# Chunk bounds of a top-k attention: PSUM transposes by TensorE replaced by 32x32 block transposes on VectorE

## The chip, the cores and the metric

The kernel runs on one core of a Trainium2 chip. The metric is device time of the whole program in microseconds (us), the median of several runs. TensorE is PE in the profile (PEld is its weight load), VectorE is DVE, ScalarE is ACT, GpSimd is POOL, and SyncE, which here issues DMAs, is SP.

## What is computed

An attention in which each query may look at six chunks of 32 keys only, followed by a gated feed-forward layer. There are 4 batches of 8 heads, 768 tokens, a head size of 64, so 24 chunks a head.

```
k_min = np.min(k_chunks, axis=3); k_max = np.max(k_chunks, axis=3)
ub = np.sum(np.maximum(q * k_min, q * k_max), axis=-1)      # per query and chunk
ub = np.where(causal, ub, -1e9)                            # chunk <= the query's own
top_chunks = np.argsort(ub, axis=-1)[..., -6:]
scores = where(selected chunk and causal, scale * q @ k.T, -1e9)
attn_out = softmax(scores) @ v
x = attn_out as (3072, 512); xn = x / rms(x) * g
out = (silu(xn @ w_gate) * (xn @ w_val)) @ w_out           # d_ff 1536
```

The bound of a chunk is written as `q . k_min + relu(q) . (k_max - k_min)`, which is two matrix products.

## The kernel before, and what sets its order

The kernel works on 16 pairs of heads, four to a batch. For a pair, k and q are loaded (`knat`, `qnat`), transposed on TensorE in fp32 ("pk" and "pq") and copied out of PSUM by ScalarE or VectorE ("kt", "qt"). VectorE reduces k over each chunk to a minimum and a maximum (`red`), their difference is taken (`diff`), and both are the stationary operand `KU` of the bounds. `relu` makes the second moving operand ("rt").

The bounds ("ub") are fp32 products of 64 rows by 32 columns, placed in the array by `tile_position`. The first four pairs (`DUO = 4`) do them one by one in `prep`: the 768 tokens are laid as three groups of 256 on three 32-column groups. Later pairs go two at a time through `duo`: four groups of 384 tokens, two for each pair. Either way a chunk's bounds then lie along partitions and tokens along the free axis. They are copied to SBUF by ScalarE or VectorE (step "ubE", tiles "ubs" and "ubd"), turned on TensorE against an identity (step "up"), and VectorE adds the causal table `cmf` (24 chunks for each token tile and head) while it takes them out of PSUM (step "ubm").

`choose` follows: twelve `max` a pair for the eight largest bounds, then two instructions that write a 0/1 selection. For pairs 0 to 3 the selection is transposed on TensorE ("st", step `selT`) and copied to `QS` by ScalarE or VectorE; later pairs write it beside q into `QN`, and two transposing DMAs from SP bring both into `QS`. The selection is extra rows of the query operand, so the score product ("sc") masks by itself. Then come exp on ScalarE ("pt"), the product with v ("av"), and VectorE's division ("xb"). When a batch's pairs are done, `norm` scales half a batch of rows ("xs", after a GpSimd power, "ri"); the first half is transposed on TensorE ("tp") and copied by ScalarE ("xT"), the others by DMA. `ffn` then runs twelve blocks of gate ("gp") and value ("vp") products and the output product ("po").

The order on each engine is not written out by hand. Every piece of work is a `Step` with an assumed cost, dependences and buffers; `Order.run` plays them through and gives an engine that is free the ready step of lowest rank. A rank is a sum of entries of `TIMES` (by pair, score block, norm and feed-forward half) and `RANK` (by kind of step). The program is then emitted in that order, and each engine works strictly down its own list. TensorE's list also has 88 "busy" products of zeros (lines 343 to 351, and 923 in `scores`), which stand where `Order.run` found nothing else to do. PSUM has eight buffers; `limits` says how many of them each sort of work may hold.

Of the kernel before, what the change touches and what calls it, by code (L numbers as in the profile page):

```python
# [21 lines left out]
GUARD = 480.0  # L22
# [5 lines left out]
        av=317.13, dif=-371.68, eps=-127.03, exp=38.25, kC=146.63, kE=47.74, kT=-378.59,  # L28
        kload=5.92, kmn=-649.18, kmx=-154.73, max=-339.88, qC=211.54, qE=806.71, qT=255.12,
        qload=7.58, relu=-70.96, root=214.18, sc=306.41, sel=71.38, selC=354.68, selT=-82.52,  # L30
        sq=-533.35, tp=81.74, tpE=457.86, ub=-353.85, ubE=-844.2, ubm=-100.58, up=-547.88,
        vload=-466.13, xT=41.94, xb=-434.88, xs=291.71,
    ),
    dict(
        av=-67.94, dif=-197.08, eps=-1181.62, exp=65.8, gate=-45.76, hh=-195.3, kC=431.48,
        kE=188.25, kT=-156.35, kload=309.73, kmn=365.65, kmx=725.58, mask=148.9, max=122.37,
        out=-321.42, po=568.17, poE=255.36, qE=-143.72, qN=503.6, qT=46.14, qX=-360.16,
        qload=286.61, relu=311.95, root=-959.29, sc=-163.03, sel=639.07, sq=-56.05, tanh=845.43,
        tg=-155.94, ub=-92.79, ubE=-119.4, ubm=322.89, up=-194.73, val=-19.16, vload=289.68,
        xT=31.48, xb=-144.92, xs=-231.75,  # L40
# [161 lines left out]
def kernel(  # L202
# [26 lines left out]
    G = 3  # L229
    DUO = 4  # L230
    KSIDE, QM = 16, 4
    HW = NT * P + D
    NPAIRS = B * NP

    SLOTS = dict(ps=8, nat=7, kb=0, qn=2, vext=4, set=3, ku=4, selq=2, qt=7, ubs=1, ubd=1, small=8, ubm=3,
# [6 lines left out]
    BOUNDS = ("ACT", "DVE")  # L242
# [78 lines left out]
    cmf = const.tile([P, NT, 2, NCH], FP32, name="cmf")  # L321
# [92 lines left out]
    def make_cmf(n):  # L414
        if n == 0:
            nc.gpsimd.memset(cmf[:], 0.0)
        for g4 in (2 * n, 2 * n + 1):
            nc.gpsimd.affine_select(
                out=cmf[32 * g4:32 * (g4 + 1)], in_=cmf[32 * g4:32 * (g4 + 1)],
                compare_op=ALU.is_ge, fill=-BIGC,  # L420
                base=g4, pattern=[[4, NT], [0, 2], [-1, NCH]], channel_multiplier=0,
            )

    c_cm = add("cmf", "POOL", 1.5, -70, lambda e: make_cmf(0), [c_e])
    c_cm = add("cmf", "POOL", 1.1, -69, lambda e: make_cmf(1), [c_cm])
# [61 lines left out]
    def prep(c, i0, nb, at, lr):  # L487
# [162 lines left out]
        def choose(last, ubm, m8):  # L650
            for j in range(0, nb, 3):
                def top(e, j=j):
                    if m8.tile is None:
                        tile_of(m8, [P, 2, NT, 8] if side_q else [P, NT, 2, 8], FP32, "m8")
                    for x in range(j, j + 3):
                        for h in range(2):
                            y = (h, x) if side_q else (x, h)
                            nc.vector.max(out=m8.tile[:, y[0], y[1], :],  # L658
                                          in_=ubm.tile[:, y[0], y[1], 0:max(8, 4 * (i0 + x) + 4)])

                last = add("max", "DVE", 0.33 + 0.05 * j, rank(at, b, "max", j, "step"), top, last, opens=[m8], uses=[ubm])
                last = [last]
            sq = None if side_q else Buf("selq")

            def pick(e):
                if side_q:
                    if side_q:
                        s12 = QN[qn.slot][:, D:D + 2 * NT * P].rearrange("p (t d) -> p t d", d=P)
                        m12, um = (x.tile[:].rearrange("p h i e -> p (h i) e") for x in (m8, ubm))
                    else:  # L670
                        s12 = SELQ[sq.slot][:, 0:nb].rearrange("p i h e -> p (i h) e")
                        m12, um = (x.tile[:, 0:nb].rearrange("p i h e -> p (i h) e") for x in (m8, ubm))
                    nc.vector.scalar_tensor_tensor(
                        out=s12[:, :, 0:NCH], in0=m12[:, :, 5:6].to_broadcast([P, 2 * nb, NCH]),
                        scalar=THRFLOOR, in1=um, op0=ALU.max, op1=ALU.is_gt)
                    nc.vector.tensor_scalar(
                        out=s12[:, :, NCH:NCH + 1], in0=m12[:, :, 0:1], scalar1=-GUARD,
                        scalar2=0.0, op0=ALU.add, op1=ALU.max)
                    return
                s12 = SELQ[sq.slot][:, 0:nb].rearrange("p i h e -> p (i h) e")  # L680
                m12 = m8.tile[:, 0:nb].rearrange("p i h e -> p (i h) e")
                nc.vector.scalar_tensor_tensor(
                    out=s12[:, :, 0:NCH],
                    in0=m12[:, :, 5:6].to_broadcast([P, 2 * nb, NCH]),
                    scalar=THRFLOOR, in1=ubm.tile[:, 0:nb].rearrange("p i h e -> p (i h) e"),
                    op0=ALU.max, op1=ALU.is_gt)
                nc.vector.tensor_scalar(
                    out=s12[:, :, NCH:NCH + 1], in0=m12[:, :, 0:1], scalar1=-GUARD,
                    scalar2=0.0, op0=ALU.add, op1=ALU.max)
# [26 lines left out]
        if p >= DUO:  # L716
            c.bound = (big["q"], rel), [rl] + [c.dif[x] for x in c.dif], choose
            return

        nq = n // G  # L720
        nj = nq // P
        ub = [Buf("ps", "prep") for _ in range(2)]
        ubs = Buf("ubs")

        def bounds(e):
            t = [tile_of(x, [P, 2 * P], FP32, "ub") for x in ub]
            for m, src in ((0, big["q"].tile), (1, rel.tile)):
                for g in range(G):
                    for h in range(2):
                        rows = slice(h * D, (h + 1) * D)  # L730
                        nc.tensor.matmul(  # L731
                            t[h][g * CH:(g + 1) * CH, 0:nq], KU[c.ku.slot][rows, m, :],
                            src[rows, g * nq:(g + 1) * nq],
                            start=(m == 0), stop=(m == 1), tile_position=(h * D, g * CH))

        um = add("ub", "PE", 0.25 + 0.8 * nq / 256, rank(at, b, "ub"), bounds,
                 [rl, df] + [c.dif[x] for x in c.dif], opens=ub,
                 uses=[c.ku, big["q"], rel])
        ue = []
        for h in range(2):  # L740
            def ub_out(e, h=h):
                if ubs.tile is None:
                    tile_of(ubs, [G * CH, 2, 2 * P], FP32, "ubs")
                evict(e, ubs.tile[:, h, 0:nq], ub[h].tile[0:G * CH, 0:nq])

            ue.append(add("ubE", "", {e: {"ACT": act(nq), "DVE": dve(nq)}[e] for e in BOUNDS},
                          rank(at, b, "ubE", h, "step"), ub_out, [um], opens=[ubs],
                          uses=[ub[h]]))
        up, ubm, m8 = Buf("ps", "prep"), Buf("ubm"), Buf("small")

        def up_turn(e):
            t = tile_of(up, [P, G, nj, 2, CH], FP32, "up")
# [406 lines left out]
```

## Time and profile before

| | us |
|---|---|
| runs | 317.39, 317.07, 317.8 (median 317.39) |
| profiled execution, first to last instruction (span) | 315.0 |
| busy TensorE / VectorE / ScalarE / GpSimd | 307.8 / 232.9 / 193.3 / 105.9 |

The profiled execution is known by its span; what a run takes around it is the difference to the runs. In a group of instructions the columns are line, engine, operation, tiles, shapes and count, then the busy time of the group in us and the mean of one instruction in ns, then the engine's idle time before them and what ended it. In the chain of waits a piece has its start, its length, the engine, tile and line, and how many instructions it merges. In the timeline a piece has start, length, engine, line, operation, shapes, count, and in brackets the idle time before it. TensorE's instructions are pipelined: the mean of one holds the way through the array, so that the distance between neighbours in the chain, not that mean, is what each costs. The granted TensorE clock was 1.000 in the whole span.

### The profile page before, as it was taken

The page shows a single profiled execution, that of the slowest core. Times are in us where ns is not written, and L with a number is a line of the kernel's source. Part 1 is how long each engine was busy: PE and PEld are TensorE (multiplying, and loading weights), DVE is VectorE, ACT ScalarE, POOL GpSimd, SP SyncE. Part 2 cuts the span into 40 slices and gives each one's busy share as a digit, 9 for nine tenths or more (in the row PEclk, how much of TensorE's full clock was granted, in tenths as well). Part 3 has the DMA queues.
Part 4 walks back from the last instruction along what each step waited for, and adds up shares of the span by engine and source line. Part 5 has one row for each costly group of instructions (what it writes and reads, how often), then busy time and mean ns, then how long its engine had stood idle before and what let it go on. Part 6 is the DMA issues. An engine that isn't in the chain of part 4 may idle for free.

```text
span 315.0 us, 7610 instructions
## 1 busy us (share of the span) xinstructions
PE 307.8 (98%) x2820; PEld 195.9 (62%) x2820; DVE 232.9 (74%) x654; ACT 193.3 (61%) x417; POOL 105.9 (34%) x160
## 2 busy tenths in 40 slices
PE   8989999899999999999999999999999999999995
PEld 4567788566667654776766667556666546555542
DVE  7679999898965964996899959558776928844600
ACT  4689997747289773479866599954348423423131
POOL 8684636017345752104802667510001200000000
PEclk9999999999999999999999999999999999999999
DMA  8999995998979997999472566650000151001023
GB/s 169 219 207 198 203 148 85 175 145 108 137 113 183 127 100 198 234 184 216 118 50 51 86 91 80 143 143 35 0 2 0 37 147 54 2 33 67 2 85 115
DMA packets 113333, 35.36 MB, mean 112 GB/s; under 512 B 106256, under 2 KB 110096, under 8 KB 113296
## 3 DMA queue, kind: packets, MB, share of 16 engines
q1 hardware_dynamic: 83184, 26.62, 42.1%
q0 software_dynamic: 28512, 7.87, 26.7%
q10 hardware_dynamic: 1600, 0.39, 0.6%
q8 instruction: 22, 0.36, 0.5%
q14 instruction: 15, 0.12, 0.2%
HBM read 28.57 MB, written 6.29 MB: 111 GB/s over the span
## 4 chain that ended last, share of the span: by engine, by line
PE 97%; ACT 2%; issue 0%; DVE 0%; ACTq 0%
PE gp L1045 20%; PE po L1086 20%; PE vp L1066 20%; PE sc L876 12%; PE av L912 7%; PE busy L346 5%; PE pk L525 4%; PE pq L525 3%; PE ub L789 3%; PE ub L731 1%; PE up L811 1%; ACT pt L893 1%; PE sc L882 1%; PE up L755 0%; PE st L702 0%; ACT xT L297 0%
## 5 line engine op out<-in xcount | busy, mean ns | idle before, releaser
L893 ACT ACTIVATE pt<-sc 128x512 bf16<-128x512 f32 (+3 forms) x192 | 87.8, 583 | 4.6 <-PE sc L876 2.8
L1052 ACT ACTIVATE sg<-gp 128x384 bf16<-128x384 f32 x96 | 47.3, 500 | 58.2 <-PE gp L1045 53.0
L1045 PE MATMUL gp<-xT,wg 128*128 128x384 bf16 x384 | 74.6, 326 | 0.9 <-ACT xT L297 0.9
L1066 PE MATMUL vp<-xT,wv 128*128 128x384 bf16 x384 | 74.8, 326 | 0.0
L1058 DVE SCALAR_TENSOR_TENSOR tg<-sg,gp 128x384 bf16<-128x384 bf16 x96 | 51.7, 548 | 21.8 <-ACT sg L1052 20.0
L1086 PE MATMUL po<-wo,hh 128*128 128x512 bf16 x288 | 66.5, 379 | 0.0
L1074 DVE TENSOR_TENSOR hh<-vp,tg 128x384 bf16<-128x384 f32 x96 | 51.2, 549 | 6.8 <-PE vp L1066 5.5
L876 PE MATMUL sc<-qs,ke 128*128 128x128 bf16 (+5 forms) x420 | 52.7, 251 | 0.1
L1045 PEld LDWEIGHTS <-wg 128*128 128x128 bf16 x384 | 36.8, 98 | 24.4 <-issue 1.7
L1066 PEld LDWEIGHTS <-wv 128*128 128x128 bf16 x384 | 36.5, 98 | 24.0 <-issue 0.6
L1086 PEld LDWEIGHTS <-hh 128*128 128x128 bf16 x288 | 27.5, 98 | 29.4
L899 POOL TENSOR_SCALAR_AFFINE_SELECT pt<-pt 128x512 bf16<-128x512 bf16 (+1 forms) x48 | 25.7, 552 | 57.3 <-ACT pt L893 57.2
L876 PEld LDWEIGHTS <-ke 128*128 128x128 bf16 (+1 forms) x420 | 30.5, 97 | 12.4 <-issue 2.1
L301 POOL CAST ke<-kt 64x768 bf16<-64x768 f32 x31 | 26.2, 846 | 26.9 <-ACT kt L297 15.1
L912 PE MATMUL av<-vx,pt 128*128 128x65 bf16 x672 | 32.5, 193 | 0.2 <-ACT pt L893 0.2
L912 PEld LDWEIGHTS <-pt 128*128 128x128 bf16 x672 | 28.7, 97 | 5.8 <-issue 0.3
L299 ACT ACTIVATE osb<-po 128x512 f32<-128x512 f32 x22 | 13.3, 606 | 29.7 <-PE po L1086 29.6
L989 DVE SCALAR_TENSOR_TENSOR xs<-xb,ri,gains 128x512 bf16<-128x512 bf16 x24 | 19.1, 835 | 5.6 <-DMA xT<-xs 5.1
L346 PE MATMUL busy<-zeros 128*128 128x512 bf16 (+1 forms) x88 | 18.7, 351 | 1.3 <-DVE zeros L341 1.3
L933 DVE TENSOR_TENSOR xb<-av,rden 128x384 bf16<-128x384 f32 (+1 forms) x34 | 18.1, 534 | 1.2
L481 POOL DMA_DIRECT2D vx<-in_v_dram x16 | 16.7, 1045 | 0.5 <-PE gp L1045 0.3
L658 DVE MAX8 m<-ubm 128x8 f32<-128x8 f32 (+2 forms) x192 | 16.8, 156 | 0.0
(85 smaller groups left out, 296.8 us busy)
## 6 DMA issues: line engine op xcount, KB each, us to landing
out_dram<-osb SPq DMA_DIRECT2D x24, 256.0 KB, 2.3
knat<-in_k_dram SPq DMA_DIRECT2D x30, 192.0 KB, 4.5
qnat<-in_q_dram SPq DMA_DIRECT2D x30, 192.0 KB, 4.7
vx<-in_v_dram POOLq DMA_DIRECT2D x16, 192.0 KB, 5.9
wg<-in_moe_w_gate_dram POOLq DMA_DIRECT2D x2, 768.0 KB, 9.0
wv<-in_moe_w_val_dram POOLq DMA_DIRECT2D x2, 768.0 KB, 10.8
wo<-in_moe_w_out_dram POOLq DMA_DIRECT2D x2, 768.0 KB, 8.4
ke<-e_all SPq DMA_DIRECT2D x4, 96.0 KB, 2.9
```

What stands on the lines that cost most here:

```text
L301: engine[e].tensor_copy(out_, in_)
L346: nc.tensor.matmul(t[:, 0:n], zeros[:, 0:P], zeros[:, 0:n], start=True, stop=True)
L876: nc.tensor.matmul(t[:, x:x + m, :].rearrange("p a b -> p (a b)"), ke[kk, kb * P:(kb + 1) * P], qs[kk, q0 * P:(q0 + m) * P], start=not tri ...
L893: nc.scalar.activation(out=t[:, 0:nn, :], in_=sc.tile[:, 0:nn, :], func=ACT.Exp, scale=SCALE)
L899: nc.gpsimd.affine_select(out=pt.tile[:, 0:nd, :], in_=pt.tile[:, 0:nd, :], compare_op=ALU.is_ge, fill=0.0, base=0, pattern=[[0, nd], [1, ...
L912: nc.tensor.matmul(av.tile[:, qi - i0, :], pt.tile[:, x, :], VX[c.v.slot][:, hl * NT + kb, :], start=(begin and m == 0), stop=(left[0] == ...
L1045: nc.tensor.matmul(t[:], wg[:, g, hs], XT[b].tile[:, g, cols], start=(g == 0), stop=(g == NP - 1))
L1052: nc.scalar.activation(out=t[:], in_=gp.tile[:], func=ACT.Tanh, scale=0.5)
L1058: nc.vector.scalar_tensor_tensor(out=t[:], in0=sg.tile[:], scalar=1.0, in1=gp.tile[:], op0=ALU.add, op1=ALU.mult)
L1066: nc.tensor.matmul(t[:], wv[:, g, hs], XT[b].tile[:, g, cols], start=(g == 0), stop=(g == NP - 1))
L1074: nc.vector.tensor_tensor(out=t[:], in0=vp.tile[:], in1=tg.tile[:], op=ALU.mult)
L1086: nc.tensor.matmul(po.tile[:], hhs[ht].tile[:, th * P:(th + 1) * P], wo[:, ht, :], start=(ht == 0), stop=(ht == NHT - 1))
```

## The change

Both ways of doing the bounds become one function, `bound`, called for a single pair (0 to 3) or for two. A column group `a` of the array now takes the tokens whose place in their 128-token tile is `32a` to `32a + 31`: the moving operand is read as six runs of 32 tokens, and the 32 chunks (24 and 8 zeros) of column group `a` land on partitions `32a` to `32a + 31` of PSUM. A transpose of each 32x32 block, which VectorE does while it reads PSUM, puts tokens on partitions and chunks on the free axis. The copies to SBUF and TensorE's turns go. The causal add is done in SBUF afterwards, only on eight chunks for each token tile: from the tile's first chunk on; what lies behind them is never looked at by the maxima, and masked later by the causal score blocks. `cmf` shrinks to eight columns. All values of `RANK` and `TIMES` are new.

```diff
-    cmf = const.tile([P, NT, 2, NCH], FP32, name="cmf")
+    cmf = const.tile([P, 8], FP32, name="cmf")
...
-    def make_cmf(n):
-        if n == 0:
-            nc.gpsimd.memset(cmf[:], 0.0)
-        for g4 in (2 * n, 2 * n + 1):
+    def make_cmf(e):
+        nc.gpsimd.memset(cmf[:], 0.0)
+        for g4 in range(4):
...
-                base=g4, pattern=[[4, NT], [0, 2], [-1, NCH]], channel_multiplier=0,
+                base=g4, pattern=[[-1, 8]], channel_multiplier=0,
...
+    def bound(cs):
+        at, b, nx = f"a{cs[-1].p}", cs[0].b, len(cs)
+        ub, ubm = [Buf("ps", "prep") for _ in range(2)], Buf("ubm")
+        side_q = cs[0].p >= QM
+        def bounds(e):
+            t = [tile_of(y, [P, nx, UW], FP32, "ub") for y in ub]
+            for m in range(2):
+                for x, c in enumerate(cs):
+                    for a in range(4):
+                        for h in range(2):
+                            rows = slice(h * D, (h + 1) * D)
+                            nc.tensor.matmul(
+                                t[h][a * CH:(a + 1) * CH, x, :].rearrange("p (t r) -> p t r", r=CH),
+                                KU[c.ku.slot][rows, m, :],
+                                c.bound[0][m].tile[rows, :].rearrange(
+                                    "d (t a r) -> d a t r", a=4, r=CH)[:, a],
+                                start=(m == 0 and x == 0), stop=(m == 1 and x == nx - 1),
+                                tile_position=(h * D, a * CH))
...
+        for h in range(2):
+            def turn(e, h=h):
...
+                if side_q:
+                    o, i = ubm.tile[:, :, h * UW:(h + 1) * UW], ub[h].tile[:]
+                else:
+                    o = ubm.tile[:, 0].rearrange("p (t h c) -> p h t c", h=2, c=CH)[:, 1 - h]
+                    i = ub[h].tile[:, 0].rearrange("p (t c) -> p t c", c=CH)
+                nc.vector.transpose(out=o, in_=i)
...
+        def causal(e):
+            for x in range(nx):
+                w = ubm.tile[:, x, 0:8]
+                w = bass.AP(w.tensor, w.offset, [
+                    w.ap[0], (UW if side_q else CH, 2), ((CH if side_q else 2 * CH) + 4, NT), (1, 8)])
+                nc.vector.tensor_tensor(
+                    out=w, in0=w, in1=cmf[:].rearrange("p (a b w) -> p a b w", a=1, b=1).to_broadcast(
+                        [P, 2, NT, 8]), op=ALU.add)
```

Here `UW` is 192 and `CH` is 32. The removed parts are the ub, ubE, up and ubm steps at the end of `prep` and the whole of `duo`, which stand above. `choose` and `pick` read the new layout (32 columns a tile and head, of which 24 are used) and keep their instructions.

More of the change, by code (lines that the diff above doesn't have):

```diff
@@ L228 @@
     W = S // 2
-    G = 3
     DUO = 4
@@ L232 @@
     HW = NT * P + D
+    UW = NT * CH
     NPAIRS = B * NP
-    SLOTS = dict(ps=8, nat=7, kb=0, qn=2, vext=4, set=3, ku=4, selq=2, qt=7, ubs=1, ubd=1, small=8, ubm=3,
+    SLOTS = dict(ps=8, nat=7, kb=0, qn=2, vext=4, set=3, ku=4, selq=2, qt=7, small=8, ubm=3,
                  pt=10, xb=2, xt=2, row=3, xs=4, ff=8, hh=31, ob=3)
@@ L420, in make_cmf @@
                 compare_op=ALU.is_ge, fill=-BIGC,
[L421 removed]
+                base=g4, pattern=[[-1, 8]], channel_multiplier=0,
             )
[L424 to L425 removed]
+    c_cm = add("cmf", "POOL", 0.8, -70, make_cmf, [c_id])
     def make_tri(e):
@@ L647, in prep, with choose @@
                  uses=[big["q"]], port=True)
-        def choose(last, ubm, m8):
+        def choose(last, ubm, x, m8):
             for j in range(0, nb, 3):
@@ L653, in top @@
                     if m8.tile is None:
-                        tile_of(m8, [P, 2, NT, 8] if side_q else [P, NT, 2, 8], FP32, "m8")
-                    for x in range(j, j + 3):
+                        tile_of(m8, [P, 2 * NT, 8], FP32, "m8")
+                    for i in range(j, j + 3):
                         for h in range(2):
[L657 to L662, printed above, removed]
+                            y = h * NT + i if side_q else 2 * i + h
+                            nc.vector.max(out=m8.tile[:, y, :],
+                                          in_=ubm.tile[:, x, y * CH:y * CH + max(8, 4 * i + 4)])
+                last = [add("max", "DVE", 0.33 + 0.05 * j, rank(at, b, "max", j, "step"), top, last,
+                            opens=[m8], uses=[ubm])]
             sq = None if side_q else Buf("selq")
@@ L714, in choose @@
             return fin
[L716 to L723, printed above, removed]
-        def bounds(e):
[L726 to L739, printed above, removed]
-        for h in range(2):
[L741 to L748, printed above, removed]
@@ L749, in prep @@
-        up, ubm, m8 = Buf("ps", "prep"), Buf("ubm"), Buf("small")
-        def up_turn(e):
-            t = tile_of(up, [P, G, nj, 2, CH], FP32, "up")
-            for j in range(nj):
-                for h in range(2):
-                    nc.tensor.transpose(
-                        t[:, :, j, h if side_q else 1 - h, :], ubs.tile[:, h, j * P:(j + 1) * P],
-                        ident_f[0:G * CH, 0:G * CH])
-        ut = add("up", "PE", 0.083 * 2 * nj, rank(at, b, "up"), up_turn, ue, opens=[up], uses=[ubs])
@@ new lines, in prep @@
+        c.bound = (big["q"], rel), [rl] + [c.dif[x] for x in c.dif], choose
+    def bound(cs):
+        at, b, nx = f"a{cs[-1].p}", cs[0].b, len(cs)
+        ub, ubm = [Buf("ps", "prep") for _ in range(2)], Buf("ubm")
+        side_q = cs[0].p >= QM
+        def bounds(e):
+            t = [tile_of(y, [P, nx, UW], FP32, "ub") for y in ub]
[11 more added lines that the diff above has]
+                                tile_position=(h * D, a * CH))
+        um = add("ub", "PE", 0.35 + 0.64 * nx, rank(at, b, "ub"), bounds,
+                 [y for c in cs for y in c.bound[1]], opens=ub,
+                 uses=[y for c in cs for y in (c.ku,) + c.bound[0]])
+        turns = []
+        for h in range(2):
+            def turn(e, h=h):
+                if ubm.tile is None:
+                    tile_of(ubm, [P, nx, 2 * UW], FP32, "ubm")
+                if side_q:
+                    o, i = ubm.tile[:, :, h * UW:(h + 1) * UW], ub[h].tile[:]
+                else:
+                    o = ubm.tile[:, 0].rearrange("p (t h c) -> p h t c", h=2, c=CH)[:, 1 - h]
+                    i = ub[h].tile[:, 0].rearrange("p (t c) -> p t c", c=CH)
+                nc.vector.transpose(out=o, in_=i)
+            turns.append(add("ubT", "DVE", 0.08 + nx * UW * 0.00106, rank(at, b, "ubT", h, "step"), turn,
+                             [um], opens=[ubm], uses=[ub[h]]))
+        def causal(e):
+            for x in range(nx):
[5 more added lines that the diff above has]
+                        [P, 2, NT, 8]), op=ALU.add)
+        last = add("ubm", "DVE", 0.27 * nx, rank(at, b, "ubm"), causal, turns + [c_cm], uses=[ubm])
@@ L826, in duo @@
         for x, c in enumerate(cs):
-            c.bound[2](done[x], ubms[x], Buf("small"))
+            c.bound[2]([last], ubm, x, Buf("small"))
     GROUPS = {
@@ L1109 @@
         load_v(c, f"l{p}")
[L1110 to L1120 removed]
+        pairs.append(c)
+        if p >= DUO and p % 2 == 0:
+            continue
+        group = pairs[-2:] if p >= DUO else [c]
+        bound(group)
+        for c in group:
+            for i0, nb in PARTS[c.p]:
+                scores(c, i0, nb, f"s{c.p}.{i0}", f"pace{min(b, 1)}", b == 0)
     for b in range(B):
```

113 lines of the change are left out of this document (17 added, 96 removed), and 30 rows, old and new, of the table TIMES.

## The prediction

> **What bounds the kernel now.** I read the page's busy shares and its chain first.
>
> ```profile
> span 315.0 us, 7610 instructions
> PE 307.8 (98%) x2820; PEld 195.9 (62%) x2820; DVE 232.9 (74%) x654; ACT 193.3 (61%) x417; POOL 105.9 (34%) x160
> PE 97%; ACT 2%; issue 0%; DVE 0%; ACTq 0%
> ```
>
> The chain that ended last is TensorE almost from end to end, so a microsecond taken from TensorE's instructions comes off the time, unless TensorE then waits instead. The timed runs are 317.39 us (median); the profiled execution spans 315.0, and the 2.4 us around the span are kept as they are. A busy share doesn't tell whether TensorE does useful work, so next come its waits, the stretch before and after the first gate product (58.03 us), and the stretches around it.
>
> ```profile
> PE busy L346 <- DVE zeros L341: 1.3, 1, 1.3
> PE gp L1045 <- ACT xT L297: 0.9, 1, 0.9
> PE pk L525 <- ACT pt L893: 0.9, 1, 0.9
> 0.00:58.03 58.03, 54.84 (x656) 39.33 (x657) 50.28 (x168) 45.70 (x95) 36.02 (x58) 1.00 1.08 173
> 58.03:315.00 256.97, 253.00 (x2164) 156.57 (x2163) 182.62 (x488) 147.60 (x322) 69.87 (x102) 1.00 0.62 99
> 40.00:50.00 10.00, 10.00 (x164) 8.36 (x170) 9.69 (x24) 9.07 (x20) 4.50 (x6) 1.00 0.75 109
> ```
>
> The columns after the stretch are PE, PEld, DVE, ACT and POOL. After 58.03 TensorE lacks 4 us of 257: there its work alone sets the time. Before 58.03 it is different: part of its work is filler (L346 multiplies zeros; all 88 fillers stand before the first gate product in both built orders), and VectorE is at 97% from 40 to 50. I call this stretch the head. What a shorter TensorE list is worth there depends on VectorE.
>
> **The change part by part, on TensorE.** The transposes called "up" go altogether. Matrix products of the bounds ("ub") keep their columns in the six joint steps and are laid out anew in the four single ones.
>
> ```profile
> L811 PE MATMUL up<-ident_f,ubd 128*128 128x128 f32 x36 | 5.2, 274 | 0.0
> L755 PE MATMUL up<-ident_f,ubs 96*128 96x96 f32 x16 | 2.0, 248 | 0.0
> 53.47 0.66 PE up L811 x6
> 11.69 0.33 PE up L755 x4
> 49.30 1.45 PE ub L789 x32
> 9.66 1.01 PE ub L731 x24
> ```
>
> Instructions overlap, so their cost is read from the chain: 0.11 us for each of the 36 and 0.083 for each of the 16, which makes 3.96 + 1.33 = 5.3 us. Each bounds instruction leaves two records. A joint step has 32 records of 384 columns, eight abreast, so four turns, in 1.45 us; a single one 24 of 256 columns, six abreast, four turns, in 1.01. The difference of 0.44 over 4 x 128 columns gives 0.86 ns a column and turn, and 0.13 us besides. The new single step has 16 instructions of 192 columns, eight abreast: four turns, 0.13 + 4 x 192 x 0.00086 = 0.79 us, 0.22 less, four times 0.9. The new joint step has 32 instructions of 192: eight turns of half the length, 1.45 again. In sum 5.3 + 0.9 = 6.2 us of TensorE. The reads step through the tokens in runs of 32; a stepped operand costs nothing in the nearest rows, so I count none:
>
> ```profile
> L882 PE MATMUL sc<-trimask,ident_b 128*128 128x512 bf16 x6 | 2.3, 380 | 0.0
> L876 PE MATMUL sc<-qs,ke 128*128 128x512 bf16 x30 | 9.4, 379 | 0.0
> ```
>
> By the list of instructions, 2.1 us of the 6.2 lie in the head (16 small transposes, the first joint step's six, the four single steps, less 0.7 of score and projection work moved forward) and 4.0 behind it.
>
> Bounds on the 6.2: if 192 columns are too short to hide the issue of twice the instructions, each of the new 256 costs what the shortest product does in the chain, about 0.031 us ("av" with 65 columns, row further down: four in 0.12); 7.9 us, less than the 11.9 that the turns already take (4 x 0.79 + 6 x 1.45), so the gain stays 6.2. If each of their 512 records costs it, ub is 15.9 and the gain falls to 2.2.
>
> **On VectorE, ScalarE and GpSimd.** Evictions of the bounds and the adds from "up" go; 32x32 transposes from PSUM and small adds come.
>
> ```profile
> L818 DVE TENSOR_TENSOR ubm<-up,cmf 128x144 f32<-128x144 f32 x24 | 6.4, 295 | 0.0
> L770 DVE TENSOR_TENSOR ubm<-up,cmf 128x288 f32<-128x288 f32 x4 | 1.8, 449 | 0.1
> L301 DVE COPY ubd<-ub 128x384 f32<-128x384 f32 x6 | 3.3, 554 | 3.5 <-PE ub L789 3.4
> L301 DVE COPY ubs<-ub 96x256 f32<-96x256 f32 x3 | 1.3, 419 | 2.4 <-PE ub L731 2.4
> L297 ACT ACTIVATE ubd<-ub 128x384 f32<-128x384 f32 x6 | 2.9, 491 | 3.5 <-PE ub L789 3.5
> L297 ACT ACTIVATE ubs<-ub 96x256 f32<-96x256 f32 x5 | 1.8, 399 | 2.7 <-PE ub L731 2.7
> L418 POOL TENSOR_SCALAR_AFFINE_SELECT cmf<-cmf 32x288 f32<-32x288 f32 x4 | 2.0, 507 | 0.3
> ```
>
> VectorE loses 24 x 0.295 + 4 x 0.449 + 6 x 0.554 + 3 x 0.419 = 13.5 us. No row shows a VectorE transpose. From below it costs what a copy of the same tile does, 0.554 for 384 columns; the two adds give 1.07 ns an element and 0.14 besides, so 0.35 for 192. From above I take two passes, 0.95 and 0.55. I take the copy's price, its nearest row: 12 x 0.554 + 8 x 0.35 = 9.4. The add over eight chunks has 96 elements, 0.24 by the same line, 16 of them 3.9. Sum 13.3: VectorE gains nothing, and ScalarE is freed of 4.7 us. GpSimd's causal table shrinks from 2.0 us and a memset to five tiny instructions, early in the head. The max and selection instructions keep their counts and sizes, and no DMA is added or removed on any queue.
>
> **The head.** Up to the first "xs" of the norm, VectorE's list is as long as before: over four single steps and the first joint one it gets 8 x 0.35 + 2 x 0.554 + 6 x 0.24 = 5.3 us and loses 3 x 0.419 + 4 x 0.449 + 0.554 = 3.6 (the old joint adds stood behind xs). In the new order two copies of the chunk pattern come to it from ScalarE (about 0.55 each, as a copy of that width), and four copies of transposed k and q (0.55 each) and one relu leave it. So this engine gives the head no microsecond, TensorE's list 2.1 at most. The last part of the head can be followed in these rows:
>
> ```profile
> 48.79 0.29 PE L912 MATMUL av<-vx,pt 128*128 128x65 bf16 x4
> 53.18 2.08 DVE L989 SCALAR_TENSOR_TENSOR xs<-xb,ri,gains 128x512 bf16<-128x512 bf16 x3 [0.40 <-POOL ri L981]
> 55.34 1.30 PE busy L346 x8
> 56.47 0.61 PE L1011 MATMUL tp<-ident_b,xs 128*128 128x128 bf16 x8
> 56.90 1.09 ACT xT L297 x2
> 48.50 0.12 PE av L912 x4
> ```
>
> From the last "av" to the gate it takes 9.24 us. The rows of xs end at 55.26, yet the eight fillers queued ahead of the last "tp" hold it until 56.47. The new order has its fillers ahead of all twelve tp. VectorE has there, ahead of xs, two transposes and two adds (1.3 us with their overlap) where one copy stood (0.5); after xs come tp and the third of three ScalarE copies, about 1.1 us later. Sum: 4.4 to the start of xs, plus 0.8, plus 2.1, plus 1.1: 8.4. So 0.8 is gained there, and of the 1.1 us of shorter work ahead of the last av I take 0.4, as VectorE is nearly full. Head: 1.2, between 0 and 2.1.
>
> **Sum.** 4.0 + 1.2 = 5.2: span 309.8, time 317.39 - 5.2 = 312.2. Its own range: 311.2 (all 6.2) to 313.9 (3.5, with a few short waits).
>
> **Rivals.** *VectorE's leg grows longer than TensorE's work beside it (slower).* Place: the selection turns ("st") of the four single pairs, which TensorE meets in its order and which nothing can pass. For pair 3 the built order, its pieces priced as in the chain, leaves 4.6 us of TensorE work from the bounds' start to st, where it was 6.7; for pair 0 6.2 against 7.2. VectorE's leg after the bounds, in rows:
>
> ```profile
> 11.52 0.56 DVE L301 COPY kt<-pk 128x384 f32<-128x384 f32 x1 [0.31 <-PE pk L525]
> 12.51 0.94 DVE L556 TENSOR_REDUCE ku<-kt 128x24 f32<-128x768 f32 x1
> 13.37 0.51 DVE L658 MAX8 m<-ubm 128x8 f32<-128x8 f32 x6
> 14.65 0.57 DVE L658 MAX8 m<-ubm 128x8 f32<-128x16 f32 x6
> 15.26 1.06 DVE L682 SCALAR_TENSOR_TENSOR selq<-m,ubm 128x288 bf16<-128x288 f32 x1
> L687 DVE TENSOR_SCALAR selq<-m x4: 184/200/811, 16.2 to 38.3; 128x12 bf16<-128x12 f32 x4
> ```
>
> For pair 3: two transposes 0.7, add 0.24, two copies 1.1, twelve max 1.1, a reduce 0.94, selection 0.64 in its fast form (0.45 is the least of L682): 4.7, and 0.8 for the bounds with 0.2 to be seen: 5.7, so 1.1 us of waiting. Where the selection's two instructions run long (1.06 and 0.81) it is 1.2 more. Four pairs at 1.7 are 6.8: 312.2 + 6.8 = 319.0. It decides from 1.3 us a pair; two-pass transposes add 0.4 to each. For it: the order is tighter at all four. Against: TensorE waited for no st before, and the list ahead of each has fillers only in part.
>
> *VectorE alone sets the head.* The evacuation went from two engines to one; with 9.69 of 10 busy, the head then shortens by nothing: 317.4 - 4.0 = 313.4. The Trainium skill says in TensorEngine Tiling (Array Packing), section PSUM Bottleneck, that packing speeds up TensorE but not the emptying of PSUM, and asks for ScalarE and VectorE both. By that rule the time is this rival's; the 97% row bears it out, the 50.28 busy of 58.03 in the whole head does not.
>
> *Weight loads show.* Twice the turns need twice the loads.
>
> ```profile
> L789 PEld LDWEIGHTS ub<-qt,ku 64*32 64x32 f32 x96 | 1.1, 104 | 1.3 <-issue 0.5 <-DVE xs L989 0.4 <-DVE ubm L818 0.2
> ```
>
> If each of the 24 added turns shows its 0.104 us load, 2.5 come back: 314.7. Against it, 0.13 us is all that a joint step of four turns has beside its columns. The Trainium skill, in TensorE: Matmul & The Clock Gate, section Part 3: Packing small matmuls, has a load overlap a running product only when its row group differs, which these turns of the same tiles would break; the trace disagrees at 384 columns by that 0.13.
>
> *The weights for the value product are late.* It follows the gate by 1.3 us in the new order, by 4.5 before.
>
> ```profile
> 49.19 0.78 POOL L445 DMA_DIRECT2D wv<-in_moe_w_val_dram  x1 [0.20 <-issue]
> 62.58 1.63 PE L1066 MATMUL vp<-xT,wv 128*128 128x384 bf16 x9
> DMA to landing us min/median/max: 9.2/10.8/12.4
> ```
>
> Issued at 49.2 and landing after 9.2 to 12.4, it comes between 58.4 and 61.6; wanted at 58.1 (gate at 56.8), it costs 0.3 to 3.5: up to 315.7.
>
> **How the numbers follow.** Forecast 0.54; slower legs 0.19; VectorE's head 0.11; weight loads 0.04; late weights 0.07; all of it cancelling 0.05. About 0.2% (0.6 us) is what a measurement of this kernel tells from no change. Faster: 0.54 + 0.11 + 0.04 + 0.07 = 0.76; same 0.05; slower 0.19. The likeliest time is 312.2; the range runs from 309.3, should the head also lose its 0.9 us waits and some filler time, to 318.0, which leaves out the upper half of the slower case.
>
> **What would show it.** Right: no "up", TensorE busy less by about 6 us, ub at 1.45 and 0.8 in the chain, first gate near 56.8, TensorE's waits below 4 us. Wrong: transposes above 0.95, waits at st of a microsecond each, vp waiting for a DMA, or score products waiting for their transposed selection behind 58 us, which now rest on a wholly new order and which no row can exclude.

## The result, and the profile after

| | us |
|---|---|
| before, five runs | 317.44 (317.07 to 317.8) |
| after, five runs | 315.27 (314.38 to 317.29) |
| ratio after to before | 0.9939, 95% interval 0.9919 to 0.9959 |
| predicted | 312.2 (309.3 to 318.0) |

The kernel is faster, by 2.2 us where 5.2 were predicted. The profiled execution of after is the slowest of its five (span 315.5, the others 312.7 to 313.6), so its span isn't to be set against the 315.0 of before, and its stretches show what can happen behind the gate rather than what usually does. First the page's busy line, the chain by engines and the waits of TensorE (us in all, how often, the longest):

```profile
span 315.5 us, 7918 instructions
PE 305.1 (97%) x2992; PEld 194.8 (62%) x2992; DVE 232.3 (74%) x653; ACT 189.7 (60%) x406; POOL 102.0 (32%) x160
PE 88%; DMA 5%; DVE 3%; ACT 1%; POOL 0%; SPq 0%; issue 0%; ACTq 0%; DVEq 0%; POOLq 0%
```

```profile
PE av L836 <- POOL pt L823: 2.5, 1, 2.5
PE sc L800 <- ACT qs L296: 1.0, 1, 1.0
PE gp L969 <- ACT xT L296: 0.9, 1, 0.9
PE st L686 <- DVE ubm L735: 0.4, 1, 0.4
```

TensorE's share of the chain fell from 97% to 88%: DMA and VectorE now hold 8% of it, and there is a new stop of 2.5 us. Where these lie is seen by stretches, cut at the first gate product (58.05, before 58.03) and around the stop. Behind the stretch and its length stand the busy times of PE, PEld, DVE, ACT and POOL, then the granted clock, the DMA share and GB/s:

```profile
0.00:58.05 58.05, 54.01 (x705) 38.72 (x705) 48.08 (x156) 45.59 (x94) 34.73 (x61) 1.00 1.09 172
58.05:315.50 257.45, 251.08 (x2288) 156.12 (x2287) 184.25 (x499) 144.08 (x312) 67.24 (x99) 0.99 0.62 99
```

```profile
94.00:95.00 1.00, 1.00 (x17) 0.60 (x14) 0.20 (x1) 0.74 (x2) 0.08 (x1) 0.77 0.66 151
95.00:98.00 3.00, 3.00 (x12) 1.52 (x11) 1.11 (x2) 2.09 (x5) 1.89 (x3) 0.51 1.18 243
98.00:99.00 1.00, 1.00 (x15) 0.74 (x13) 0.56 (x1) 0.49 (x1) 0.00 (x0) 1.00 1.52 172
```

So the head kept its length, and behind it TensorE stands 6.4 us where it stood 4.0, and runs at half its clock for about 3.4 us after the stop: 0.23 + 3 x 0.49 = 1.7 us lost.

**The parts, as the chain and the groups show them.**

```profile
9.33 0.81 PE ub L714 x32
51.60 1.46 PE ub L714 x64
```

```profile
L735 DVE STREAM_TRANSPOSE ubm<-ub 128x384 f32<-128x384 f32 x12 | 6.3, 560 | 2.7 <-PE ub L714 2.7
L735 DVE STREAM_TRANSPOSE ubm<-ub 128x192 f32<-128x192 f32 x8 | 2.6, 384 | 2.1 <-PE ub L714 2.1
L745 DVE TENSOR_TENSOR ubm<-ubm,cmf 128x96 f32<-128x96 f32 x16 | 4.2, 290 | 0.2
L671 DVE TENSOR_SCALAR selq<-m x4: 189/742/814, 14.8 to 38.2; 128x12 bf16<-128x12 f32 x4
```

The bounds cost 0.81 and 1.46 us a step. The transposes cost about what a copy does (0.560 us in the mean for 384 columns, where the copy of before had 0.554, and 0.384 for 192). The three figures of the last row are least, median and most in ns. This instruction (L671, here called the guard) is the second of the two that write the selection. It changed without being touched: its median was 200 ns and is 742.

**The head.** The last "av" ahead of the norm and the first gate product, in the timeline:

```profile
49.90 0.29 PE L836 MATMUL av<-vx,pt 128*128 128x65 bf16 x4
58.05 1.46 PE L969 MATMUL gp<-xT,wg 128*128 128x384 bf16 x8 [0.93 <-ACT xT L296]
```

From av to gate it is 8.15 us (9.24 before), but av is 1.1 us later (48.79 before). To see where that is lost, take the last of the four turns of a selection ("st", pair 3) as a mark, first before, then after:

```profile
38.76 0.50 PE L702 MATMUL st<-ident_b,selq 128*128 128x128 bf16 x6
39.05 0.51 PE L686 MATMUL st<-ident_b,selq 128*128 128x128 bf16 x6
```

Of the 1.1 us, 0.3 are lost ahead of st and 0.8 between st and av. Ahead of st the chain leaves TensorE. These are the last pieces of pair 3's leg in it; the pair's bounds end on TensorE at 33.1:

```profile
36.17 0.49 DVE m L655 x6
36.66 0.85 DVE ku L553
37.51 0.75 DVE selq L668
38.26 0.74 DVE selq L671
38.99 0.07 DVE rden L856
39.06 0.49 PE st L686 x6
```

The two instructions of the selection take 1.49 us there. In the order of before the same two of the same pair were short:

```profile
37.94 0.46 DVE L682 SCALAR_TENSOR_TENSOR selq<-m,ubm 128x288 bf16<-128x288 f32 x1
38.31 0.21 DVE L687 TENSOR_SCALAR selq<-m 128x12 bf16<-128x12 f32 x1
```

In the new order two of GpSimd's casts run beside them:

```profile
37.12 0.82 POOL L300 CAST qn<-qnat 128x768 bf16<-128x768 f32 x1
37.89 1.05 POOL L300 CAST ke<-kt 64x768 bf16<-64x768 f32 x1
```

The Trainium skill (SBUF — State Buffer, section Who interferes with whom) has VectorE's tensor_scalar among the operations that can take the port pair shared with GpSimd, whoever comes second waiting for a whole instruction. These rows agree in size, 0.19 alone and 0.8 beside a cast of 0.8 to 1.05.

Between st and the last av it is ScalarE that is full. The stretch before, then after, with busy times in the same columns as above:

```profile
38.76:48.79 10.03, 10.03 (x162) 8.87 (x159) 9.40 (x23) 9.54 (x22) 3.53 (x5) 1.00 0.93 128
39.05:49.90 10.85, 10.69 (x148) 9.05 (x149) 8.99 (x20) 10.66 (x25) 4.61 (x8) 1.00 0.75 131
```

ScalarE is busy for 10.66 of 10.85 us (9.54 of 10.03 before). By its timeline it makes five copies of transposed k and q there (2.5 us) where it made two (1.0). No run moves these copies back, so that they are the cause of the 0.8 us is argued, not shown.

**The stop at 90.8 us.** GpSimd's timeline, with what ended its idle time in brackets, then TensorE's:

```profile
80.06 0.84 POOL L447 DMA_DIRECT2D wo<-in_moe_w_out_dram  x1
82.12 0.82 POOL L300 CAST qn<-qnat 128x768 bf16<-128x768 f32 x1 [1.22 <-DVE hh L998]
86.94 1.21 POOL L823 TENSOR_SCALAR_AFFINE_SELECT pt<-pt 128x512 bf16<-128x512 bf16 x2 [4.00 <-ACT pt L817]
91.77 0.82 POOL L300 CAST qn<-qnat 128x768 bf16<-128x768 f32 x1 [3.62 <-DMA qs<-qn]
92.55 0.99 POOL L823 TENSOR_SCALAR_AFFINE_SELECT pt<-pt 128x512 bf16<-128x512 bf16 x2
```

```profile
90.54 0.22 PE L800 MATMUL sc<-qs,ke 128*128 128x128 bf16 x1
93.23 0.42 PE L836 MATMUL av<-vx,pt 128*128 128x65 bf16 x8 [2.48 <-POOL pt L823]
```

TensorE wants pt, which GpSimd masks (L823). GpSimd stands 3.62 us in front of a cast of q for a later pair (8), which can't overwrite its buffer before a transposing DMA has read it; the masks are queued behind. That DMA is in the chain:

```profile
81.58 10.07 DMA qs<-qn
```

It was issued 1.5 us after the load of wo (80.06) and took 10.07 us where the median of the 24 is 4.2. In the order of before such a cast stood waiting too, but the masks behind it weren't due yet, and waited for exp (pt of ACT) themselves:

```profile
80.98 0.82 POOL L301 CAST qn<-qnat 128x768 bf16<-128x768 f32 x1 [1.33 <-DMA qs<-qn]
...
90.80 1.00 POOL L899 TENSOR_SCALAR_AFFINE_SELECT pt<-pt 128x512 bf16<-128x512 bf16 x2 [1.18 <-ACT pt L893]
91.76 0.81 POOL L301 CAST qn<-qnat 128x768 bf16<-128x768 f32 x1
```

### The profile page after: what moved, and what is told of

Its sections match the earlier page's. It is cut to its first block, busy times and chain, and to the rows that moved or that the text cites. A ratio compares the mean times of both kernels' runs of the same rounds, so it can differ in the third digit from the quotient of the medians.

```text
span 315.5 us, 7918 instructions
## 1 busy us (share of the span) xinstructions
PE 305.1 (97%) x2992; PEld 194.8 (62%) x2992; DVE 232.3 (74%) x653; ACT 189.7 (60%) x406; POOL 102.0 (32%) x160
## 4 chain that ended last, share of the span: by engine, by line
PE 88%; DMA 5%; DVE 3%; ACT 1%; POOL 0%; SPq 0%; issue 0%; ACTq 0%; DVEq 0%; POOLq 0%
PE po L1010 20%; PE vp L990 19%; PE gp L969 18%; PE sc L800 10%; PE av L836 5%; PE busy L345 5%; PE pk L522 3%; DMA qs<-qn 3%; PE pq L522 3%; PE ub L714 3%; DMA knat<-in_k_dram 2%; PE sc L806 1%; DVE m L655 1%; PE st L686 1%; DVE xb L857 1%; ACT xT L296 1%
## 5 line engine op out<-in xcount | busy, mean ns | idle before, releaser
L990 PE MATMUL vp<-xT,wv 128*128 128x384 bf16 x384 | 78.2, 330 | 0.0
L969 PE MATMUL gp<-xT,wg 128*128 128x384 bf16 x384 | 76.8, 326 | 0.9 <-ACT xT L296 0.9
L998 DVE TENSOR_TENSOR hh<-vp,tg 128x384 bf16<-128x384 f32 x96 | 52.2, 552 | 6.8 <-PE vp L990 3.9
L823 POOL TENSOR_SCALAR_AFFINE_SELECT pt<-pt 128x512 bf16<-128x512 bf16 (+1 forms) x48 | 25.9, 560 | 43.2 <-ACT pt L817 43.1
L836 PE MATMUL av<-vx,pt 128*128 128x65 bf16 x672 | 35.3, 193 | 2.5 <-POOL pt L823 2.5
L836 PEld LDWEIGHTS <-pt 128*128 128x128 bf16 x672 | 31.0, 98 | 10.6 <-POOL pt L823 2.8
L345 PE MATMUL busy<-zeros 128*128 128x512 bf16 (+1 forms) x88 | 19.3, 352 | 1.3 <-DVE zeros L340 1.3
L913 DVE SCALAR_TENSOR_TENSOR xs<-xb,ri,gains 128x512 bf16<-128x512 bf16 x24 | 18.0, 790 | 0.4 <-POOL ri L905 0.4
L856 DVE RECIPROCAL rden<-av 128x6 f32<-128x6 f32 (+1 forms) x34 | 6.4, 188 | 16.0 <-PE av L836 15.8
```

The source lines that it names most:

```text
L345: nc.tensor.matmul(t[:, 0:n], zeros[:, 0:P], zeros[:, 0:n], start=True, stop=True)
L823: nc.gpsimd.affine_select(out=pt.tile[:, 0:nd, :], in_=pt.tile[:, 0:nd, :], compare_op=ALU.is_ge, fill=0.0, base=0, pattern=[[0, nd], [1, ...
L836: nc.tensor.matmul(av.tile[:, qi - i0, :], pt.tile[:, x, :], VX[c.v.slot][:, hl * NT + kb, :], start=(begin and m == 0), stop=(left[0] == ...
L969: nc.tensor.matmul(t[:], wg[:, g, hs], XT[b].tile[:, g, cols], start=(g == 0), stop=(g == NP - 1))
L990: nc.tensor.matmul(t[:], wv[:, g, hs], XT[b].tile[:, g, cols], start=(g == 0), stop=(g == NP - 1))
L998: nc.vector.tensor_tensor(out=t[:], in0=vp.tile[:], in1=tg.tile[:], op=ALU.mult)
```

## The experiments

Two things were to be explained: the stop behind the gate, and a head that gained nothing. "Before" differs from chip to chip (medians 316.24, 316.87 and 317.5 in the three groups of runs), so times are compared within a group. The first group is c_after, e_cast, e_wo and h_fill; the second m_alone, h_noguard and h_turn; the third e_cast2, h_act and e_guard.

**c_after: the changed kernel once more**, as a base.

> The changed kernel unaltered, as the mark for the runs beside it. In its profile av waited 2.5 us for a GpSimd mask near 91 us, and the TensorE clock was granted at 0.76 to 0.82 from 92 to 100 us. If that wait belongs to the order of the instructions, it is here again, between 1.5 and 3.5 us; if it was an accident of one execution, it is absent and the profiled span is near 311.

315.31 us (314.49 to 317.04, ten executions), ratio 0.9982 [0.9959, 1.0004]; the two measurements of the change meet at 0.996, and this one alone doesn't tell the change from none. The stop is there and shorter, and the clock did not fall after it in the profiled execution:

```profile
PE av L836 <- POOL pt L823: 1.2, 1, 1.2
PE pk L522 <- DMA knat<-in_k_dram: 0.8, 2, 0.5
```

Its ten executions fall in two groups: four with a mean clock of 0.995 have spans of 314.7 to 315.3, six with 0.997 to 1.000 of 312.8 to 313.8. A mean of 0.995 is also what the two profiled executions with a half clock behind the stop have (after, and h_turn below), and the 1.7 us that it costs are of the size of that distance. The length of the stop went with the load: here wo lands at 89.69 and the transposing DMA at 90.58, in the first profile at 90.74 and 91.65, 1.1 us later, and the stop is 1.3 longer.

**e_cast: the cast behind the masks.** Nothing else is moved.

```diff
     done = order.run(PLACE)
...
+    late = done.pop(place_of("qN", "a8"))
+    done.insert(place_of("mask", "s7.0", 7.0) + 1, late)
```

> One GpSimd cast of q (for the pair 8) is put behind the six masks that followed it in the list; nothing else is moved. Theory A (the cast waits for a transposing DMA and the mask queued behind it holds av and so TensorE): the wait near 91 us is gone, no drop of the clock, and the time is 2 to 4 us below the changed kernel's. Rival B (TensorE finds the next late thing, for instance score products that wait for their transposed selection): the wait reappears within 20 us and the time is within 0.7 us of the changed kernel's.

312.94 us (312.92 to 313.65), ratio 0.9897 [0.9878, 0.9915]: 2.4 us less than the changed kernel beside it. TensorE's wait for pt is gone, and the cast now stands behind the masks:

```profile
58.03:311.20 253.17, 248.40 (x2274) 155.54 (x2287) 184.27 (x499) 143.76 (x312) 67.29 (x99) 1.00 0.62 100
```

```profile
94.89 0.99 POOL L823 TENSOR_SCALAR_AFFINE_SELECT pt<-pt 128x512 bf16<-128x512 bf16 x2 [0.66 <-ACT pt L817]
95.83 0.81 POOL L300 CAST qn<-qnat 128x768 bf16<-128x768 f32 x1
```

The stretch behind the gate is 253.17 against 256.97 before: 3.8 us shorter, where the prediction had 4.0. These two profiles are of different chips; by the medians of its own group the gain over before is 3.3 us. The held cast had taken 2.4 of it.

**e_wo: the load of wo later**, so that the transposing DMA isn't issued beside it.

```diff
     done = order.run(PLACE)
...
+    late = done.pop(place_of("wo", "w3"))
+    done.insert(place_of("mask", "s5.0", 7.0) + 1, late)
```

> The first of the two loads of w_out on GpSimd's queue is put behind that cast and two masks; the cast and the masks keep their order. Theory A1 (the transposing DMAs of the selection are held up by the 786 KB load that was issued just before them): they land within 5 us of their issue instead of 10, the cast is not held, and the time is 2 to 4 us below the changed kernel's. Rival A2 (they are slow because of the v and q loads and of their own number): they still take 8 us or more, av still waits over 1.5 us, and the time is within 0.7 us of the changed kernel's.

316.38 us (315.32 to 318.65), ratio 1.0001 [0.9975, 1.0028]: the mechanism came as expected, the time didn't. The profiled execution kept its clock; five of the ten have a mean clock of 0.992 to 0.995, so that in them it seems to have fallen as in c_after. Issue and landing of the transfers around the load, from the trace (us):

```
changed kernel                      e_wo
wo    80.06 -> 90.74                qs   80.20 -> 82.70
qs    80.31 -> 90.94                qs   81.47 -> 85.95
qs    81.58 -> 91.65                wo   90.39 -> 99.14
qnat  83.04 -> 92.54                knat 90.82 -> 99.51
qnat  83.75 -> 93.35                knat 91.45 -> 101.49
```

Without the load in flight the same transposing DMAs land after 2.5 and 4.5 us, and the cast isn't held (87.99). But what is issued behind the load lands behind it here too, and now it is k that TensorE waits for:

```profile
PE pk L522 <- DMA knat<-in_k_dram: 2.8, 2, 2.4
```

The wait moved from the mask to k. The Trainium skill (DMA: Bandwidth & Descriptors, section Queues, rings and completion order) says that a transfer's completion is written only after every earlier write of the same DMA engine, across its queues. Both columns agree: of the transfers shown, none that was issued after the load landed before it. No run here tells that order from a plain sharing of the DMA engines.

**h_fill: half the columns in all 88 fillers.** If TensorE's list set the head, 6 us less of it would show.

```diff
-            nc.tensor.matmul(t[:, 0:n], zeros[:, 0:P], zeros[:, 0:n], start=True, stop=True)
+            nc.tensor.matmul(t[:, 0:n // 2], zeros[:, 0:P], zeros[:, 0:n // 2], start=True, stop=True)
```

> Each of the 88 filler products has half its columns; the order stays. It takes about 7 us from TensorE's list ahead of the first gate product (now at 58.05 us). Theory H (VectorE's and ScalarE's work sets the head): the gate moves by less than 1.5 us and TensorE's idle time ahead of it grows by 5 us or more. Rival P (TensorE's list sets it): the gate comes 4 to 7 us earlier. A granted clock below 0.97 in the head would spoil the reading.

```profile
L345 PE MATMUL busy<-zeros 128*128 128x256 bf16 (+1 forms) x88 | 13.3, 281 | 1.7 <-DVE zeros L340 1.3 <-DVE ubm L735 0.3
```

The fillers' busy time fell from 19.3 to 13.3 us, and the first gate product stayed at 58.06. Up to there TensorE stands 8.3 us where it stood 4.0. Time 314.75 (313.21 to 315.78), ratio 0.9947 [0.9912, 0.9981]. TensorE's list doesn't set the head; a shorter one waits more. (The last st came 0.5 us later in this run, at 39.58, and the way from it to the gate was 0.5 shorter, so up to 0.5 of the 6 us may have counted.)

**m_alone: the new bounds in the old order.** The kernel before, all ranks kept, with the new products, transposes and adds put in the places of the old steps; the place of "up" stays in the order, empty.

```diff
-            t = [tile_of(x, [P, 2 * P], FP32, "ub") for x in ub]
...
+            lay_bounds([c], [(big["q"], rel)], [tile_of(x, [P, 1, UW], FP32, "ub") for x in ub])
...
-                evict(e, ubs.tile[:, h, 0:nq], ub[h].tile[0:G * CH, 0:nq])
+                turn_block(own, 1, side_q, h, ub[h])
...
+            add_causal(own[0], 0, side_q)
```

> The kernel before with its own order of steps, into which only the new bounds are put: new layout and eight-chunk table, a VectorE transpose where each copy of a bound stood (on VectorE also where ScalarE had made the copy), nothing where the TensorE turns stood, one add where two stood. All ranks are the old ones. Theory A (the saving on TensorE is real behind the gate, the head is set by VectorE and ScalarE): the gate stays within 0.7 us of 58.0, the five joint turns behind it bring 3.3 us, the time is 2.5 to 3.8 us below the kernel before. Rival B (the gain belongs to the new ranks, and the transposes in one engine's list cost what they save): within 0.7 us of the kernel before, or above it.

316.44 us (315.95 to 317.79), ratio 0.9995 [0.9976, 1.0014]: nothing. The first gate product is at 57.54, 0.5 us earlier than before. Behind it TensorE is busy for 251.60 us (253.00 before) but stands 7.0 (4.0 before), with waits at many places (its span is 316.1, those of the other nine are 314.2 to 316.0):

```profile
PE pq L564 <- DMA qnat<-in_q_dram: 1.4, 2, 1.1
PE av L902 <- DMA vx<-in_v_dram: 1.1, 1, 1.1
PE sc L866 <- DVE qs L301: 0.6, 1, 0.6
```

So the gain needs the new ranks, and the ranks brought the stop with them. (The new ranks without the new bounds weren't tried, so how much ranks alone would give is open.)

**h_noguard and h_turn: VectorE shorter and longer in the head.** The first leaves out the guard of pairs 0 to 3 (2.5 us of VectorE), the second makes their transposes twice (2.6 us more).

```diff
+                if side_q:
                     nc.vector.tensor_scalar(
                         out=s12[:, :, NCH:NCH + 1], in0=m8.tile[:, :, 0:1], scalar1=-GUARD,
...
-                nc.vector.transpose(out=o, in_=i)
+                for _ in range(1 if side_q else 2):
+                    nc.vector.transpose(out=o, in_=i)
```

> The changed kernel without the second selection instruction of the pairs 0 to 3 (the guard column, 128x12): VectorE's list gets shorter by four instructions that took 0.8, 0.2, 0.7 and 0.8 us ahead of the selection turns, 2.5 us in all. The guard stays zero. Theory H (VectorE's leg between the bounds and the selection turn sets the head): the gate comes 0.8 to 2.5 us before 58.05 and the two waits at 33 to 36 us (0.4 for the selection turn, 1.0 for the scores) shrink. Rival P (TensorE's list): within 0.3 us of 58.05.

> The changed kernel with the two transposes of each of the pairs 0 to 3 done twice: VectorE's list gets 2.6 us longer in the head, with the other lists as they are. Theory H: the gate comes 1.3 to 2.6 us later than 58.05, TensorE waits by as much more. Rival P: within 0.5 us of 58.05.

The first gate product comes at 57.44 and 59.16, against 58.05: 0.6 earlier and 1.1 later, so 0.24 and 0.42 us for each us of these instructions. VectorE's busy time, in which overlap counts once, is 230.8 and 235.7 against 232.3: by it the two are 0.41 and 0.33. (The runs with the head unaltered have their gate at 57.95 to 58.23.) VectorE is in the path of the head, but only for part of it; both came in under what was expected. Times, one execution each, are 313.84 and 317.81. Only 1.7 us of that distance lie ahead of the gate; behind it h_noguard has a stop of 1.6 us and a full clock after it, h_turn one of 2.3 and then half the clock.

**e_cast2, h_act, e_guard: ScalarE's share, and a guard that leaves VectorE.** All three have the moved cast. h_act makes ScalarE's relu of pairs 0 to 3 twice (three times 0.85 us); e_guard gives the guard of these pairs to GpSimd.

```diff
-                nc.scalar.activation(out=t[:, 0:n], in_=big["q"].tile[:, 0:n], func=ACT.Relu)
+                for _ in range(1 if side_q else 2):
+                    nc.scalar.activation(out=t[:, 0:n], in_=big["q"].tile[:, 0:n], func=ACT.Relu)
...
-                nc.vector.tensor_scalar(
+                (nc.vector if side_q else nc.gpsimd).tensor_scalar(
                     out=s12[:, :, NCH:NCH + 1], in0=m8.tile[:, :, 0:1], scalar1=-GUARD,
```

> The changed kernel with GpSimd's cast of q for pair 8 behind the masks, once more, as the base of the two kernels that run beside it. If the held cast was the whole cause of the stop at 90 us, 312.9 us again (312.5 to 313.4), the first gate product at about 58.0 us, no wait for pt of GpSimd above 0.5 us. If the first measurement was luck of the transfers, 314.5 to 315.5 as the changed kernel has.

> The kernel with the moved cast; in pairs 0 to 3 the relu of the transposed q on ScalarE is made twice, 3 x 0.85 = 2.6 us more of ScalarE in the head, nothing else. Theory J (VectorE and ScalarE set the head in turns, a leg passes from one to the other): the first gate product comes 0.6 to 1.4 us later, the time is 313.5 to 314.3 us. Theory V (VectorE alone sets the head, ScalarE has slack in it): gate moves by less than 0.3 us, time 312.9 to 313.2 us.

> The kernel with the moved cast; the guard instruction of the selection of pairs 0 to 3 (0.8 us where it runs beside GpSimd, 2.5 us in all) is made by GpSimd instead of VectorE. If VectorE's leg can be shortened this way, the gate comes 0.3 to 0.6 us earlier, as without the guard, and the time is 312.3 to 312.6 us. Rival: the selection then waits for GpSimd's queue (casts of 0.8 to 0.9 us in it) and the casts behind it wait for the maxima; the gate stays or comes up to 1 us later, 312.9 to 313.9 us.

| | us | ratio to before | first gate product |
|---|---|---|---|
| e_cast2 | 314.04 (313.18 to 315.02) | 0.9900 [0.9867, 0.9932] | 58.01 |
| h_act | 313.65 (313.61 to 314.44) | 0.9895 [0.9865, 0.9924] | 59.04 |
| e_guard | 312.26 (312.26 to 312.81) | 0.9847 [0.9823, 0.9870] | 57.37 |

The ratio of the moved cast is the same as in the first group, with a wider spread of its four executions (spans 311.5 to 313.3, all at a clock of 1.000) that no profile here explains. h_act moves the gate by 1.0 us for 2.6 of ScalarE: 0.40. Its time doesn't show it, within that spread. e_guard is the quickest kernel of all: 5.2 us less than before. (That this is the size of the forecast is chance: moving the cast and the guard was no part of it.) On GpSimd the guard takes 0.52 us instead of 0.62 on VectorE, and st waits 0.3 us for it:

```profile
L671 POOL TENSOR_SCALAR selq<-m 128x12 bf16<-128x12 f32 x4 | 2.1, 522 | 0.9 <-DVE m L655 0.9
```

Together: a us of fillers on TensorE's list is worth 0 to 0.1 at the gate, one on VectorE's 0.24 to 0.42, one on ScalarE's 0.40. In after, h_noguard, h_turn, h_act and e_guard the gate comes 18.8 to 19.0 us behind the last st (39.05, 38.63, 40.17, 40.05 and 38.56), so what these runs changed acted almost wholly ahead of that st. This fits a head set by a path that goes from VectorE to TensorE to ScalarE and back, where no engine alone is the bound; the copies on ScalarE behind st no run tests.

## Why the prediction was half right

- **TensorE's saving, 6.2 us: right.** No "up" is left; a single step costs 0.81 us (0.79 predicted), a joint one 1.46 (1.45). Of the 4.0 put behind the gate, 3.8 come out once the cast is moved (3.3 by the times within that group).
- **VectorE's prices: nearly right.** The transposes cost about the copy's price (0.560 against 0.554, the shorter 0.384 against 0.35) and the add 0.290 against 0.24, in sum 14.4 us where 13.3 were predicted. VectorE's busy time is the same (232.9 before, 232.3 after).
- **The head, 1.2 us: wrong, it gained 0.** The part from the last av to the gate was right (8.15 against 8.4). The step that failed is the one before it: "of the 1.1 us of shorter work ahead of the last av I take 0.4". That av came 1.1 us later instead. This price rested on TensorE's list getting shorter, and a us of that list is worth next to nothing there. The busy times of VectorE and ScalarE in the whole head did not grow (48.08 and 45.59 us against 50.28 and 45.70), but two legs did. Ahead of the last st the prediction took pair 3's selection "in its fast form", 0.64 us; it fell beside GpSimd's casts and took 1.49, and st came 0.3 us later than before. Without the guard, or with it on GpSimd, the gate comes 0.6 earlier. Between st and av, 0.8 us more, the prediction looked at VectorE alone: it counted four copies of k and q as leaving that engine and ScalarE as freed of 4.7 us, but the copies went to ScalarE (21 of them in the whole head, 15 before), which is full in this stretch. That this is why av is late is not tested. The gain of 1.1 behind av only made up for this. The rival "VectorE alone sets the head" has the right price (no gain) and half the cause. What the prediction quotes beside it from the Trainium skill (TensorEngine Tiling (Array Packing), section PSUM Bottleneck), that packing speeds up TensorE and not the emptying of PSUM, fits the price; but VectorE, which alone takes the bounds out of PSUM now, is busy for less of the head than before.
- **Behind the gate: the path was missing.** The prediction said that "no DMA is added or removed on any queue", which is true, and so didn't look at what the new ranks do to GpSimd's queue. There a cast that waits for a transposing DMA got ahead of masks that TensorE waits for: 2.5 us in the profiled execution, 1.2 in another. The final warning, of scores that wait for their transposed selection, named the right DMA but the wrong reader: what waited wasn't the score but the next writer of the DMA's source, and all that stood behind it on its engine.
- **The clock: not in the prediction at all.** It was 1.000 throughout before, and fell to half for 3.4 us after the 2.5 us stop. In the profiled execution this makes the sum whole: 309.8 predicted, 1.2 for the head, 2.5 for the stop and 1.7 for the clock are 315.2 of 315.5. In that of c_after, nearer to the median, 309.8, 1.2, a stop of 1.2 and 0.8 of waits for k are 313.0 of 313.4.
- **The time beside the span.** The 2.4 us kept around the span mixed a quick profiled execution with the median of others. In the runs of after time and span of the same execution differ by 1.7 to 1.8 us (317.29 and 315.5; 315.27 and 313.6).
- **The other rivals didn't come.** st waited 0.4 us in all, not 1.7 a pair (the long selection of that rival did come for pair 3, but as a longer leg); the loads of the shorter products don't show (0.81 and 1.46 us a step); the value product didn't wait for its weights.

## What to carry to other kernels

When ranks or an order change, work that leaves one engine's list can arrive in another's: look at that list too, in the stretch where the work lands. Then go through every engine's queue, the light ones as well: for each instruction that waits for a DMA or for a buffer to be read, ask what stands behind it and who waits for that. A filled TensorE list isn't a bound where it is filled with fillers; half their length is a cheap test of it. A small instruction moved off the engine that a leg waits for (the guard) gave 0.6 us at the gate, where the whole rewrite had given nothing, and moving a load out of one queue's way can put it in another's.

## What the runs showed that was not expected

A stop of TensorE can cost more than its length: after 2.48 us the granted clock was 0.77, 0.51 and 1.00 in the stretches 94 to 95, 95 to 98 and 98 to 99. It isn't a matter of length alone. In h_turn a stop of 2.25 us was followed by the same (first row), in e_wo one of 2.36 by none (the others), nor was one of 1.6 in h_noguard or 1.2 in c_after:

```profile
95.00:98.00 3.00, 3.00 (x21) 1.77 (x19) 0.75 (x2) 2.27 (x4) 1.97 (x3) 0.50 1.10 238
101.62 0.85 PE L522 MATMUL pk<-ident_f,knat 128*128 128x128 f32 x6 [2.36 <-DMA knat<-in_k_dram]
102.00:105.00 3.00, 3.00 (x28) 2.11 (x27) 2.82 (x5) 2.49 (x7) 1.82 (x3) 1.00 1.23 196
```

The Trainium skill (TensorE: Matmul & The Clock Gate, Part 1: The HAM clock gate) knows half speed after an idle window of about 3.4 us that runs free of the program; the half agrees with 0.51, while the stops that sufficed here were shorter than such a window. What decides between the two cases isn't shown. Moreover, a transposing DMA of 2.5 to 4.5 us takes 8.8 to 10.6 when it is issued right after a load of 768 KB (after and c_after, against e_wo).
